# Two up-weight loads moved to GpSimd's queue, and the 384-column output store to ScalarE's

## Chip, core and metric

One Trainium2 chip, one core of it. The metric is the device time of one execution in microseconds (us). In the text, PE is TensorE, ACT is ScalarE, DVE is VectorE, POOL is GpSimd and SP is SyncE; "SPq" in a row of the profile is SP's queue, where it issues a transfer.

## What is computed

A parallel block: a layer norm of `x` (2048 rows of 512), then the sum of `x`, a diagonal state-space layer A and a gated feed-forward layer B. All inputs are bf16, accumulation is in f32.

```python
def reference(A_x, ..., B_w_gate, B_w_up, B_w_down):
    x = A_x
    xn = _layernorm(x, axis=-1)
    ...
    # A: Bu = xn @ B_bar.T ; h_t = Lam_bar * h_(t-1) + Bu_t over 2048 steps ; y = 2 Re(h @ C.T) + xn * Dskip
    # B: (gelu(xn @ w_gate) * (xn @ w_up)) @ w_down, with 512 -> 1376 -> 512
    return x + A(xn) + B(xn)
```

## The kernel before

**Tiling.** The 2048 rows are four blocks `b` of 512, each of four tiles `j` of 128 rows. The feed-forward width of 1376 is eleven tiles of 128 (the last has 96), the model width of 512 is four steps `k` of 128. Per block the kernel forms the normalised transposed rows `XNT`, gate and up products with gelu (`GU`, L842), the state inputs (`BU`, L748), the scan on DVE (`CHAIN`), and the down product together with the states' output product (`DN`, L883).

**Order of the work.** The program records every operation with an assumed duration and the buffers it reads and writes. A planner (`Sched`) then places operations: PE and SP keep the order in which they were recorded, DVE, ACT and POOL are ordered by a simulation of the assumed durations and by explicit `order_behind` links. `emit` writes each engine's list out with semaphore waits; each transfer has a semaphore of its own.

**The first block is special.** It does not wait for transposed normalised rows. Tile by tile, DVE subtracts the mean (`cent`, L960: 128 columns, then 384; for tiles 2 and 3 `sub`, L949), PE transposes the centred tile (`cent_T`, L683), ACT copies it out of PSUM (L688), and PE multiplies it, one `k` step at a time, with the first 512 columns of the gate and up weights (`GT_k`, L700). So the first 512 columns come in eight loads of 128 KB, one for gate and one for up per step `k` (`ld_wk`, L485 to L488, issued in the loop at L500 to L504): here they are called G0, U0, G1, U1, G2, U2, G3, U3, after the step counted from 0. The "steps 2 and 3" of the change's name are U1 and U2 in this count. PE's order at the start is written out by hand (L966 to L1012): transposes of tile 0, transposes of tile 1, tile 0 with G0, with U0, tile 1 with G0, with U0, tile 0 with G1, tile 0 with U1, transposes of tile 2, and so on.

**Queues at the start.** SP issues, one behind the other: `x` tile 0, G0, U0, G1, U1, G2, U2, `x` tile 3, G3, U3, then four larger loads with the other columns of the gate and up weights (L505, L506, L529, L530), a small transpose of the parameters (L514) and the transposes of the normalised rows (L735). ACT issues `x` tiles 1 and 2 and three parameter rows. POOL issues no transfer; it fills constants: an index matrix for the identity (L474), a zero row block (L476), and in the order of the plan a 4-column constant (L541), the index row `IOTJ` of 512 int32 (L477, read by DVE's tables much later), and more constants (L543, L544, L542). DVE makes the identity (`IDN`, L475).

**The end.** The last tile of 128 rows is made in two parts of 384 and 128 columns (`DN(3, tail=384)`, L911 to L920). For each part DVE adds the skip term on the way out of PSUM (`evO`, L901), and SP issues the store (L903). Before the 384-column store SP waits for the landing of all but the last four stores (L336 to L338), and behind the last store for those four (L342, L343).

Of the kernel before, what the change touches and what calls it, by code (L numbers as in the profile page):

```python
# [77 lines left out]
class Sched:  # L78
# [212 lines left out]
    def emit(self):  # L291
        nc, es = self.nc, self.es
        order = self.order
        esem = {}
        for e in ENGINES:
            if any(op.kind == "eng" for op in order[e]):
                esem[e] = es.enter_context(nc.semaphore("q_" + e))
        cnt = {e: 0 for e in ENGINES}
        nd = 0
        for e in ENGINES:  # L300
            for op in order[e]:
                if op.kind == "eng":
                    cnt[e] += 1
                    op.sem, op.val = esem[e], cnt[e]
                else:
                    op.sem, op.val = es.enter_context(nc.semaphore("d%d" % nd)), 16
                    nd += 1
        self.n_sems = len(esem) + nd
        plan = {}
        nwait = 0  # L310
        for e in ENGINES:
            seen = {}
            prog = []
            for op in order[e]:
                need = {}
                for d in op.deps:
                    if d.eng == e and (d is op.behind or d.kind == "eng" and e == "tensor"):
                        continue
                    key = ("e", d.eng) if d.kind == "eng" else ("d", d.id)
                    if seen.get(key, 0) >= d.val:  # L320
                        continue
                    if key not in need or need[key].val < d.val:
                        need[key] = d
                for key, d in need.items():
                    seen[key] = d.val
                waits = [(d.sem, d.val) for d in need.values()]
                nwait += len(waits)
                prog.append((waits, op))
            plan[e] = prog
        self.n_waits = nwait  # L330
        final_waits = [(op.sem, 16) for op in sorted(self.out_ops, key=lambda o: o.finish)]

        for e in ENGINES:
            h = getattr(nc, e)
            for n, (waits, op) in enumerate(plan[e]):
                if e == "sync" and n == len(plan[e]) - 2:  # L336
                    for (s, v) in final_waits[:-4]:
                        h.wait_ge(s, v)  # L338
                for (s, v) in waits:
                    h.wait_ge(s, v)  # L340
                op.fn(h).then_inc(op.sem, 1 if op.kind == "eng" else 16)
        for (s, v) in final_waits[-4:]:  # L342
            nc.sync.wait_ge(s, v)  # L343


# [13 lines left out]
def d_dve_ts4x(n): return 220.0 + 0.26 * n  # L359
D_TINY = 160.0  # L360
def d_act(n, ptr=0): return 190.0 + 0.833 * n + 90.0 * ptr
# [3 lines left out]
def build(nc, ins, out):  # L365
    with ExitStack() as es:
        E = es.enter_context
        S = Sched(nc, es)
# [10 lines left out]
        WU = A.alloc("WU", [KD, F], BF16)  # L379
# [5 lines left out]
        WUc = [Buf("WUc%d" % i, "sbx", 100 + 10 * i, 101 + 10 * i) for i in range(KD + 2)]  # L385
# [34 lines left out]
        PROW = A.alloc("PROW", [128], BF16)  # L420
        PROW16 = Buf("PROW16", "sb", PROW.lo, PROW.hi, PROW.ap[0:16, :])
        PROWq = [Buf("PROW%d" % q, "prow", q, q + 1) for q in range(3)]
# [31 lines left out]
        IOTJ = A.alloc("IOTJ", [512], I32, at=OUTB_all.lo)  # L454
# [11 lines left out]
        POOL = lambda fn, dur, r, w, tag="", after=(): S.op("gpsimd", fn, dur, r, w, tag, after)  # L466
        PE = lambda fn, dur, r, w, tag="": S.op("tensor", fn, dur, r, w, tag)

        GATE = {"before_gelu": [], "nh": 0}
# [3 lines left out]
        GATE["table"] = ACT(lambda e: e.activation(SCR.ap, HALF.ap[:, 0:1], ACTF.Gelu_apprx_tanh), 100, [HALF], [SCR], "gelu0")  # L473
        POOL(lambda e: e.iota(IOT.ap, [[1, 128]], base=0, channel_multiplier=-1), 300, [], [IOT], "iota")  # L474
        GATE["ident"] = V(lambda e: e.tensor_scalar(IDN.ap, IOT.ap, 0.0, None, ALU.is_equal), d_dve_ts4x(128), [IOT], [IDN], "ident")  # L475
        POOL(lambda e: e.memset(PROW16.ap, 0.0), 100, [], [PROW, *PROWq], "prow0")  # L476
        GATE["iotj"] = POOL(lambda e: e.iota(IOTJ.ap, [[1, 512]], base=0, channel_multiplier=0), 600, [], [IOTJ], "iotj")  # L477
        NM0, NM1 = (A.alloc(n, [1], F32) for n in ("NM0", "NM1"))

        def ld_x(b):  # L480
# [1 line left out]
                X_all.ap[:, 4 * b:4 * b + 4, :], x2[512 * b:512 * (b + 1), :].rearrange("(j p) d -> p j d", p=128)),  # L482
                512 * 1024, writes=X[4 * b:4 * b + 4], tag="ld_x%d" % b)

        def ld_wk(W, Wc, src, k):  # L485
            f0, f1 = FC[0]
            return S.dma(lambda e: e.dma_start(W.ap[:, k, f0:f1], src[128 * k:128 * (k + 1), f0:f1]),  # L487
                         256 * (f1 - f0), writes=[Wc[k]], tag="ld_w")  # L488

        def ld_w(W, Wc, src, n):  # L490
            f0, f1 = FC[n]
            return S.dma(lambda e: e.dma_start(W.ap[:, :, f0:f1], src[:, f0:f1].rearrange("(k p) f -> p k f", p=128)),
                         1024 * (f1 - f0), writes=[Wc[KD + n - 1]], tag="ld_w")

        def ld_x0(j, queue="sync", after=()):
            return S.dma(lambda e, j=j: e.dma_start(X[j].ap, x2[128 * j:128 * (j + 1), :]), 128 * 1024, writes=[X[j]], tag="ld_x0", queue=queue, after=after)  # L496
# [3 lines left out]
        for k in range(KD):  # L500
            if k == 3:
                ld_x0(k)
            ld_wk(WG, WGc, ins["B_w_gate"], k)
            ld_wk(WU, WUc, ins["B_w_up"], k)  # L504
        ld_w(WG, WGc, ins["B_w_gate"], 1)  # L505
        ld_w(WU, WUc, ins["B_w_up"], 1)  # L506

# [39 lines left out]
        def next_bank():  # L547
            b_ = rstate["n"] % 8
            rstate["n"] += 1
            return b_  # L550
# [316 lines left out]
        def DN(b, split=False, tail=None):  # L867
            k2, k3 = b % 2, b % 3
            banks = [next_bank() for _ in range(4)]
            xbank = next_bank() if tail else None  # L870

            def seed(j, c0=0, c1=D):
                tt, bank = 4 * b + j, banks[j]
                bank = banks[j] if c0 == 0 else xbank
                ACT(lambda e: e.activation(PS[bank][:, c0:c1], X[tt].ap[:, c0:c1], ACTF.Copy), d_act(c1 - c0), [X[tt]], [BANK[bank]], "seed")  # L875

            def mms(j, ops, last, rds, c0, c1):
                bank = banks[j] if c0 == 0 else xbank

                def f(e):  # L880
                    ins_ = None
                    for n, (l_, r_) in enumerate(ops):
                        ins_ = e.matmul(PS[bank][:, c0:c1], l_[:, 128 * j:128 * (j + 1)], r_[:, c0:c1], start=False,  # L883
                                        stop=last and n == len(ops) - 1, skip_group_check=True)
                    return ins_
                PE(f, d_pe([c1 - c0] * len(ops)), rds + [BANK[bank]], [BANK[bank]], "DN%d" % b)

            def hidden(j, c0=0, c1=D):
                ops = [(HTt[k2][ft].ap[0:FROWS[ft], :], WD.ap[0:FROWS[ft], ft, :]) for ft in range(KF)]
                mms(j, ops, False, [HTt[k2][ft] for ft in range(KF)] + WDc, c0, c1)  # L890

            def states(j, c0=0, c1=D):
                ops = [(SSc[k3][s][c].ap, CT[c][s].ap) for s in range(KP) for c in range(2)]
                mms(j, ops, True, [SSs[k3][s] for s in range(KP)] + [CT[c][s] for c in range(2) for s in range(KP)], c0, c1)

            def store(j, c0=0, c1=D):
                tt = 4 * b + j
                bank = banks[j] if c0 == 0 else xbank
                ko = tt % 4
                ob = OUTB[ko] if c1 - c0 == D else Buf("OUTBp%d" % c0, "sb", OUTB[ko].lo + 2 * c0, OUTB[ko].lo + 2 * c1)  # L900
                V(lambda e: e.tensor_tensor(OUTB[ko].ap[:, c0:c1], PS[bank][:, c0:c1], XD[tt].ap[:, c0:c1], ALU.add),  # L901
                  d_dve_1x(c1 - c0), [BANK[bank], XD[tt]], [ob], "evO")
                S.dma(lambda e: e.dma_start(out[0, 128 * tt:128 * (tt + 1), c0:c1], OUTB[ko].ap[:, c0:c1]),  # L903
                      256 * (c1 - c0), reads=[ob], is_output=True, tag="st_out")

            if split:
                for j in range(4):
                    seed(j); hidden(j)
                for j in range(4):
                    states(j); store(j)  # L910
            elif tail:  # L911
                for j in range(3):
                    seed(j); hidden(j)
                for j in range(3):
                    states(j); store(j)
                parts = ((0, tail), (tail, D))
                for c in parts:
                    seed(3, *c)
                for c in parts:
                    hidden(3, *c); states(3, *c); store(3, *c)  # L920
            else:
                for j in range(4):
                    seed(j); hidden(j); states(j); store(j)
# [183 lines left out]
```

## Time and profile before

| what | us |
|---|---|
| median of 3 runs (lowest, highest) | 177.25 (176.7, 177.45) |
| the profiled execution | 177.24 |
| its span, first to last instruction | 175.9 |
| outside the span (177.24 - 175.9) | 1.3 |
| PE busy | 171.8 (98%) |
| DVE busy | 159.6 (91%) |
| ACT busy | 95.7 (54%) |
| POOL busy | 10.7 (6%) |

The profile is one execution on the chip. Its page gives busy times per engine, the span cut in 40 slices, the queues of the transfers, and the chain of work that ended last, which is followed back from the last instruction to whatever released each step. The trace behind the page answers narrower questions: the instructions of one stretch of time, who waited for whom, and the transfers that were issued in a stretch with the time to their landing. PE is busy for 98% of the span, so time can only be gained where PE stands idle (before its first real matmul and in short gaps), behind its last matmul, or by giving it less work.

### The profile page before, as it was taken

Reading aid. Unit: us, or ns where it says so; the run is one execution under the profiler, and the core shown is the slowest. Engines: PE = TensorE matmul, PEld = TensorE weight load, DVE = VectorE, ACT = ScalarE, POOL = GpSimd, SP = SyncE. Lnnn points to the kernel's source line nnn. Section 1 sums busy time; section 2 is a strip of 40 time slices with the busy share of each in tenths; the row PEclk is TensorE's granted clock in tenths of the full one; section 3 lists DMA queues with packets and bytes.
Section 4 is the critical chain, followed back from the end, with each engine's and each line's share of the span. In section 5 each row is a group of like instructions: output and inputs, shape, how many; then the busy total and the mean of one; then the engine's idle time right before and its main releaser. Section 6 shows DMA issues by size and latency. Waiting matters only on the chain.

```text
span 175.9 us, 2506 instructions
## 1 busy us (share of the span) xinstructions
PE 171.8 (98%) x874; PEld 84.5 (48%) x889; DVE 159.6 (91%) x279; ACT 95.7 (54%) x187; POOL 10.7 (6%) x24
## 2 busy tenths in 40 slices
PE   8899999999999999999999999999999999999995
PEld 2545464844544444444644444444464444444453
DVE  5977999997989989889899999989999899999931
ACT  5376677999766898383576792000667960000000
POOL 3212120210000000002100000000000000000000
DMA  5999999695999000002025000002001000000221
GB/s 174 259 314 186 248 212 121 120 133 108 182 287 232 10 0 2 0 30 88 5 42 109 0 0 0 4 0 89 30 0 30 4 0 0 0 0 0 95 95 56
DMA packets 32421, 14.37 MB, mean 82 GB/s; under 512 B 23736, under 2 KB 32408, under 8 KB 32408
## 3 DMA queue, kind: packets, MB, share of 16 engines
q1 hardware_dynamic: 32096, 13.94, 35.6%
q10 hardware_dynamic: 312, 0.27, 0.5%
q8 instruction: 7, 0.11, 0.3%
q14 instruction: 6, 0.05, 0.1%
HBM read 6.46 MB, written 2.10 MB: 49 GB/s over the span
## 4 chain that ended last, share of the span: by engine, by line
PE 95%; DMA 2%; SPq 1%; issue 1%; DVE 0%
PE PS L883 37%; PE PS L842 32%; PE PS L748 16%; PE PS L711 4%; PE PS L816 3%; PE PS L700 2%; DMA arena<-in_B_w_up_dram 2%; SPq L487 1%; PE PS L683 0%; SPq L496 0%; DVE arena L901 0%
## 5 line engine op out<-in xcount | busy, mean ns | idle before, releaser
L883 PE MATMUL PS<-arena 128*128 128x512 bf16 (+3 forms) x317 | 65.9, 366 | 0.3
L842 PE MATMUL PS<-arena 128*128 128x512 bf16 x257 | 57.1, 379 | 0.4
L883 PEld LDWEIGHTS PS<-arena 128*128 128x128 bf16 (+1 forms) x323 | 30.9, 98 | 35.2
L842 PEld LDWEIGHTS PS<-arena 128*128 128x128 bf16 x264 | 25.7, 98 | 30.3
L786 DVE TENSOR_TENSOR_SCAN arena<-arena 128x512 bf16<-128x512 f32 x32 | 38.9, 1254 | 0.0
L857 ACT ACTIVATE arena<-PS 128x512 bf16<-128x512 f32 x33 | 19.8, 599 | 26.2 <-DVE arena L901 16.7
L748 PE MATMUL PS<-arena 128*128 128x512 bf16 (+1 forms) x142 | 28.1, 355 | 0.1
L861 ACT ACTIVATE arena<-PS 128x512 bf16<-128x512 f32 x33 | 19.8, 599 | 5.4 <-PE PS L842 5.4
L748 PEld LDWEIGHTS PS<-arena 128*128 128x128 bf16 x144 | 14.1, 98 | 13.3
L875 ACT ACTIVATE PS<-arena 128x512 f32<-128x512 bf16 (+2 forms) x17 | 9.6, 581 | 19.7 <-DVE arena L901 19.0
L757 ACT ACTIVATE arena<-PS 128x512 bf16<-128x512 f32 x32 | 17.5, 596 | 1.8 <-PE PS L748 1.8
L901 DVE TENSOR_TENSOR arena<-PS,arena 128x512 bf16<-128x512 f32 (+2 forms) x17 | 10.9, 652 | 6.4 <-PE PS L883 6.3
L863 DVE TENSOR_TENSOR arena<-arena 128x512 bf16<-128x512 bf16 x33 | 13.2, 416 | 2.2 <-ACT arena L861 2.0
L775 DVE TENSOR_TENSOR arena<-arena 128x4096 bf16<-128x4096 bf16 (+1 forms) x5 | 9.2, 1859 | 0.4 <-ACT arena L610 0.4
L798 DVE TENSOR_TENSOR arena<-arena 128x4096 bf16<-128x4096 bf16 x4 | 9.2, 2288 | 0.1
L773 DVE TENSOR_TENSOR arena<-arena 128x4096 bf16<-128x4096 bf16 (+1 forms) x5 | 9.2, 1857 | 0.0
L799 DVE TENSOR_TENSOR arena<-arena 128x4096 bf16<-128x4096 bf16 x4 | 9.1, 2284 | 0.0
L720 ACT ACTIVATE arena<-PS,arena 128x256 bf16<-128x256 f32 (+1 forms) x16 | 6.5, 450 | 4.1 <-PE PS L700 2.4
L614 DVE BATCH_NORM_STATS2 arena<-arena 128x6 f32<-128x512 bf16 x12 | 7.8, 680 | 0.0
L711 PE MATMUL PS<-arena 128*128 128x512 bf16 (+1 forms) x40 | 7.1, 336 | 0.0
L723 DVE SCALAR_TENSOR_TENSOR arena<-PS,arena 128x256 bf16<-128x256 f32 (+1 forms) x16 | 6.3, 443 | 0.8 <-PE PS L700 0.8
L700 PE MATMUL PS<-arena 128*128 128x512 bf16 (+1 forms) x30 | 6.1, 337 | 0.5 <-DMA arena<-in_B_w_up_dram 0.5
(95 smaller groups left out, 123.6 us busy)
## 6 DMA issues: line engine op xcount, KB each, us to landing
out_dram<-arena SPq DMA_DIRECT2D x15, 128.0 KB, 1.7
arena<-in_A_x_dram SPq DMA_DIRECT2D x3, 512.0 KB, 5.5
arena<-in_B_w_down_dram SPq DMA_DIRECT2D x1, 1280.0 KB, 8.8
arena<-in_B_w_gate_dram SPq DMA_DIRECT2D x4, 128.0 KB, 3.3
arena<-in_B_w_up_dram SPq DMA_DIRECT2D x4, 128.0 KB, 3.6
arena<-in_B_w_gate_dram SPq DMA_DIRECT2D x1, 480.0 KB, 6.8
arena<-in_B_w_up_dram SPq DMA_DIRECT2D x1, 480.0 KB, 7.7
arena<-arena SPq DMA_TRANSPOSE x25, 2.9
```

Source lines behind the costliest of these rows:

```text
L700: PE(lambda e: e.matmul(dst, XCd(j, k), WGU[:, ws[0]:ws[-1] + 1, k, f0:f1], start=first, stop=k == KD - 1, skip_group_check=True), d_pe([w ...
L711: ins_ = e.matmul(dst, XCd(j, k), WGU[:, :, k, f0:f1], start=(k == 0), stop=(k == KD - 1))
L748: ins_ = e.matmul(PS[bank][:, 128 * j0:128 * j1], BBT[c][dk].ap[:, 128 * s:128 * (s + 1)], XNT[b].ap[:, dk, 128 * j0:128 * j1], start=(dk ...
L757: GATE["evBu"] = ACT(lambda e, bank=bank, k3=k3, s=s, c=c: e.activation(SSc[k3][s][c].ap, PS[bank][:, :], ACTF.Copy), d_act(512), [BANK[ba ...
L786: V(lambda e, g=g, rb=rb, init=init: e.tensor_tensor_scan(g.ap, rb, g.ap, init, ALU.mult, ALU.add), d_dve_scan(512), [g, PA[RRr]] + ([CARc ...
L842: ins_ = e.matmul(PS[bank][0:m, c0:c1], W.ap[:, dk, 128 * ft:128 * ft + m], XNT[b].ap[:, dk, c0:c1], start=(dk == 0), stop=(dk == KD - 1))
L857: GATE["last_gelu"] = ACT(lambda e, bg=bg, kk=kk, m=m: e.activation(GG[kk].ap[0:m, :], PS[bg][0:m, :], ACTF.Gelu_apprx_tanh), d_act(512), ...
L861: ACT(lambda e, bu=bu, kk=kk, m=m: e.activation(UPB[kk].ap[0:m, :], PS[bu][0:m, :], ACTF.Copy), d_act(512), [BANK[bu]], [UPB[kk]], "evU")
L863: V(lambda e, kk=kk, m=m, ft=ft, k2=k2: e.tensor_tensor(HTt[k2][ft].ap[0:m, :], GG[kk].ap[0:m, :], UPB[kk].ap[0:m, :], ALU.mult), d_dve_tt ...
L875: ACT(lambda e: e.activation(PS[bank][:, c0:c1], X[tt].ap[:, c0:c1], ACTF.Copy), d_act(c1 - c0), [X[tt]], [BANK[bank]], "seed")
L883: ins_ = e.matmul(PS[bank][:, c0:c1], l_[:, 128 * j:128 * (j + 1)], r_[:, c0:c1], start=False, stop=last and n == len(ops) - 1, skip_group ...
L901: V(lambda e: e.tensor_tensor(OUTB[ko].ap[:, c0:c1], PS[bank][:, c0:c1], XD[tt].ap[:, c0:c1], ALU.add), d_dve_1x(c1 - c0), [BANK[bank], XD ...
```

## The change

Three things are edited. No instruction of PE or DVE is added, removed or reordered.

1. U1 and U2 are issued from POOL's queue, behind the zero row block (L476) and in this order, instead of from SP's. In the changed program POOL's list is: index matrix, zero row block, load U1, load U2, the 4-column constant, the index row `IOTJ`, and the other constants. SP's list loses two entries near its front: `x` tile 0, G0, U0, G1, G2, `x` tile 3, G3, U3, and so on.
2. The store of the 384-column part is issued from ACT's queue, where it is the last instruction. The 128-column store stays on SP.
3. SP's waits for landed stores are split anew: before its last store but one (a full tile of the last block) it waits for the first 12 of the 17 stores, before its last store (128 columns) for the next three, each set closed by a no-op, and behind the last store there is one instruction that waits for both parts of the last tile.

```diff
@@ emit
-                if e == "sync" and n == len(plan[e]) - 2:
-                    for (s, v) in final_waits[:-4]:
+                if e == "sync" and n >= len(plan[e]) - 2:
+                    for (s, v) in (final_waits[:-5] if n < len(plan[e]) - 1 else final_waits[-5:-2]):
                         h.wait_ge(s, v)
+                    h.nop(nofuse=True)
                 for (s, v) in waits:
                     h.wait_ge(s, v)
                 op.fn(h).then_inc(op.sem, 1 if op.kind == "eng" else 16)
-        for (s, v) in final_waits[-4:]:
+        for (s, v) in final_waits[-2:]:
             nc.sync.wait_ge(s, v)
@@ build
-        POOL(lambda e: e.memset(PROW16.ap, 0.0), 100, [], [PROW, *PROWq], "prow0")
-        GATE["iotj"] = POOL(lambda e: e.iota(IOTJ.ap, [[1, 512]], base=0, channel_multiplier=0), 600, [], [IOTJ], "iotj")
+        GATE["swdge"] = POOL(lambda e: e.memset(PROW16.ap, 0.0), 100, [], [PROW, *PROWq], "prow0")
...
-        def ld_wk(W, Wc, src, k):
+        def ld_wk(W, Wc, src, k, queue="sync"):
             f0, f1 = FC[0]
             return S.dma(lambda e: e.dma_start(W.ap[:, k, f0:f1], src[128 * k:128 * (k + 1), f0:f1]),
-                         256 * (f1 - f0), writes=[Wc[k]], tag="ld_w")
+                         256 * (f1 - f0), writes=[Wc[k]], tag="ld_w", queue=queue)
...
             ld_wk(WG, WGc, ins["B_w_gate"], k)
-            ld_wk(WU, WUc, ins["B_w_up"], k)
+            if k == 0:
+                ld_wk(WU, WUc, ins["B_w_up"], k)
+            else:
+                op_ = ld_wk(WU, WUc, ins["B_w_up"], k, "gpsimd" if k < 3 else "sync")
+                if k < 3:
+                    GATE["swdge"] = S.order_behind(op_, GATE["swdge"])
+        S.order_behind(POOL(lambda e: e.iota(IOTJ.ap, [[1, 512]], base=0, channel_multiplier=0), 600, [], [IOTJ], "iotj"), GATE["swdge"])
...
                 S.dma(lambda e: e.dma_start(out[0, 128 * tt:128 * (tt + 1), c0:c1], OUTB[ko].ap[:, c0:c1]),
-                      256 * (c1 - c0), reads=[ob], is_output=True, tag="st_out")
+                      256 * (c1 - c0), reads=[ob], is_output=True, tag="st_out", queue="scalar" if c1 - c0 == tail else "sync")
```

## The prediction

> **What bounds the kernel now.** I read the chain that ended last first, because PE is busy for 98% of the span and only what stands outside PE's work can be saved. These are the two ends of that chain; the columns are start, duration and what ran.
>
> ```profile
> 1.66 0.42 SPq L487
> 2.08 0.04 issue
> 2.12 0.43 SPq L487
> 2.56 0.04 issue
> 2.60 3.94 DMA arena<-in_B_w_up_dram
> 6.54 0.05 issue
> 6.58 0.39 PE PS L700 x2
> ...
> 173.91 0.02 issue
> 173.93 0.29 DVE arena L901
> ```
>
> Until 6.58 the end of the kernel hangs on U1, issued at 2.60 and landed at 6.54; after it the chain is PE without a break to 173.91, then the last `evO` and its store. PE's timeline shows how much there is at the front: eight matmuls from 5.00 (four steps of two), then a stop.
>
> ```profile
> 5.00 1.10 PE L700 MATMUL PS<-arena 128*128 128x256 bf16 x8
> 6.58 0.39 PE L700 MATMUL PS<-arena 128*128 128x256 bf16 x2 [0.48 <-DMA arena<-in_B_w_up_dram]
> ```
>
> The eight end at 6.10, the last of them lasts 0.27 and so starts at 5.83. Two neighbours stand 0.12 apart (6.58 to 6.97, the second also 0.27 long), so the U1 step could have begun at 5.95. **At most 6.58 - 5.95 = 0.63 us is to be had there.** Next the tail, SP's queue beside DVE's last two additions (mean ns behind the bar):
>
> ```profile
> 173.97 0.33 SPq L903 DMA_DIRECT2D out_dram<-arena  x1
> ```
> ```profile
> 174.35 0.42 SPq L903 DMA_DIRECT2D out_dram<-arena  x1
> ```
> ```profile
> L901 DVE TENSOR_TENSOR arena<-PS,arena 128x384 bf16<-128x384 f32 x1 | 0.6, 558 | 2.8 <-PE PS L883 2.8
> L901 DVE TENSOR_TENSOR arena<-PS,arena 128x128 bf16<-128x128 f32 x1 | 0.3, 293 | 0.1
> ```
>
> The 128-column sum is ready at 173.93 + 0.29 = 174.22, but SP is issuing the 384-column store until 174.30 and starts the last one at 174.35.
>
> **The tail, worked out.** An unhindered store follows its addition closely: the store at 170.59 follows an addition that ran from 169.87 for 0.69, so 0.03 behind. The last store could start at 174.22 + 0.03 = 174.25 instead of 174.35: **0.10 us earlier**, and the end of the span, its landing 1.5 later, with it. ACT's new last instruction has nothing behind it, and ACT's row before ends at 162.72 + 0.28 = 163.00, so nothing is delayed. That store leaves at 173.87 + 0.03 = 173.90 and lands 1.6 later (the 96 KB row), 175.5, ahead of the last at 174.25 + 1.5 = 175.75; ACT's loads at the start took 2.3 where SP's took 2.2, which does not close the 0.25. The waits cost nothing on either side: before the last store they ask for three stores of which the latest left at 170.59 and lands 1.7 later, at 172.3, 1.9 us before it matters. The closing wait that goes lay in the 1.5 us of landing. Bounds: 0 to 0.10; I take 0.10, since the row at 170.59 is the same kind of store on the same queue.
>
> **The front, worked out.** SP's issues stand 0.47 apart (2.12, 2.60, 3.08). So G1 keeps 2.12, G2 moves from 3.08 to 2.60, `x` tile 3 from 4.03 to 3.08, G3 and U3 and the larger loads forward by two issues, 0.95. None of these was awaited: U2 landed at 3.55 + 3.7 = 7.25 for a step that PE starts about 8.3, U3 at 4.98 + 3.5 = 8.5 for one at 9.6 (the 7th and the 13th of the matmuls that stand 0.22 apart from 7.04). The transposes behind them gain little, since L735 waits for DVE's normalised rows (9.11 + 0.41 = 9.52, now issued at 9.74).
>
> U1 itself leaves POOL behind the zero block (1.01 + 0.20 = 1.21), not at 2.60. That is not 1.39 us of gain, because the transfers were not waiting for issue. Here are the busy tenths of the DMA engines in 0.2 us slices from 0 to 8:
>
> ```profile
> DMA  0000000005699999999998999986788999997699
> ```
>
> From 2.2 us on they are full. Landings follow one another at the pace of the transfers: U0 at 1.66 + 3.3 = 4.96, G1 at 2.12 + 3.2 = 5.3, G2 at 3.08 + 3.8 = 6.9, U2 at 7.25, so about 0.37 per 128 KB. U1 alone is out of step, 1.2 behind G1, of which 0.83 is excess. Without it U1 would have landed at 6.54 - 0.83 = 5.71. In the changed kernel U2 is in flight early too and takes its 0.37 before the four loads U0, G1, U1, U2 are through, so the last of what PE needs, now probably G1 on SP's queue, lands at 5.71 + 0.37 = 6.08. PE then does G1's two matmuls (0.22) and, 0.04 behind the landing as before, reaches U1's step at 6.08 + 0.04 + 0.22 = 6.34: **0.24 earlier**. From 6.58 on PE's own work follows without gaps, and things that PE does not feed have more room than that: `sub` of tile 3 ends at 8.56 + 0.35 = 8.91 for a transpose at 9.84, the fourth transpose of L735 lands about 13.8 + 2.9 = 16.7 for products at 18.29.
>
> The price of a POOL issue is not in this trace. Below, ACT's shortest issue is 0.27 and SP's 0.43; above, the longest issue at the start is SP's transpose with 2.03. I take 0.87, POOL's own costliest instruction (L621), because it is POOL that has to do the work: U1 is issued by 2.08, U2 by 2.95, and the constants that took POOL from 1.21 to 2.36 now run from 2.95 to 4.11. POOL's next need is at 7.58, after 5.2 us of idle time, and the index row's reader starts at 17.3, so lateness on POOL itself is free up to 4 us. If an issue were as cheap as SP's, constants end at 3.2; at 2.03, at 6.4.
>
> What may not be free is DVE. While POOL filled its constants before, this stood on DVE, against 254 ns for the 128-column form of L960:
>
> ```profile
> 1.10 1.23 DVE L475 TENSOR_SCALAR arena<-arena 128x128 bf16<-128x128 int32 x1
> ```
>
> It ended with POOL's run (2.33 against 2.36). Later, L949 took its usual 0.35 at 8.56 beside two POOL instructions of one or three columns. So wide POOL fills may hold such an operation up, small ones did not. In the changed kernel the fills meet the `cent` operations (3.48 to 3.96, 4.17 to 4.65), which feed PE: a hold until 4.11 puts them and all of PE's start 0.63 late, and U1's step to 5.95 + 0.63 = 6.58, no gain at all. I take no hold for the forecast, as the type of L475 differs from that of `cent`.
>
> The Trainium skill speaks against this change in two places. "SBUF — State Buffer", Who interferes with whom, says that a DVE operation in a two-port mode (`tensor_scalar` can be one) and a POOL operation exclude each other, and that a transfer issued from GpSimd waits for its descriptors meanwhile; L475 agrees with it and L949 at 8.56 does not show it. By that rule the hold above would be the forecast, 177.14. "DMA: Bandwidth & Descriptors", Issuing engines are not separate DMA queues, says that another issuer saves issue time alone; by that rule only the order at the engines counts, and the front gives 0 to 0.24.
>
> **Sum.** 177.24 (profiled, 175.9 of span and 1.3 around it; the median is 177.25) - 0.24 - 0.10 = **176.90**.
>
> **Rivals.**
> - *The wait moves to another load, or the hold eats the gain.* U1 and U2 get ahead, G1 or U0 is late; or the fills hold `cent` for 0.63. The excess of 0.83 can strike G1 as well as U1. For it: full DMA engines, a fixed number of bytes. Time: 177.24 - 0.10 = 177.1, within 0.2.
> - *POOL holds DVE for longer (the other side).* Its place is the first `cent` at 3.48, and it decides from a hold of 0.63 on. A whole constant run of 1.16 in front of it gives 5.95 + 1.16 = 7.11 for U1's step: 177.24 + 0.53 - 0.10 = 177.7. With issues of 2.03 that keep DVE out until 1.21 + 4.06 = 5.27, the hold is 1.79 and the time 177.24 + 1.16 - 0.10 = 178.3. For it: L475. Against it: 5.27 needs both the dearest issue and a hold by work that no row shows.
> - *The whole stop goes.* U1 early, G1 by 5.6: 0.63 + 0.10, 176.5. Against it: G1 would have to land as before although two more loads compete.
> - *The change does nothing at the front* because POOL's transfers start late: with 2.03 for each issue U1 leaves POOL at 3.24 and lands, with the 3.5 us that such loads took at the start, at 6.7: 177.24 + 0.2 - 0.10 = 177.3.
>
> **Chances.** Forecast (176.7 to 177.05) 0.40; the stop gone 0.15; no net gain at the front (177.05 to 177.4, with POOL's late start) 0.25; POOL in DVE's way, up to 178.1, 0.10, and beyond 0.10. A measurement of this kernel can tell about 0.5%, 0.9 us, from no change (its three runs differ by 0.75). Even the whole 0.73 stays inside that; with scatter, 0.04 for faster by over 0.5%. Slower by over 0.5% is the last case, 0.10; within 0.5% 0.86. The range runs from 176.4, the whole gain and a little scatter, to 177.9, which leaves out the worst of POOL's case.
>
> **What would show it.** Right: PE's first L700 step on U1 begins between 6.0 and 6.5 with the remaining stop put down to a gate load, and SP's last store starts 0.03 behind `evO`. Wrong: a stop before the first L683, or L960 rows well over 254 and 314 ns (hold); POOL's issue rows over 2 us; the last landing that of ACT's store; or a stop that now comes later, at the transposes of tile 3.

## The result, and the profile after

| | before | changed |
|---|---|---|
| median of 22 runs (lowest, highest) | 177.27 (176.7, 179.28) | 178.47 (177.66, 187.0) |
| ratio, 95% interval | | 1.006 (1.004 to 1.0081) |
| median span / median time outside the span (before: over the 34 runs beside the repeat below) | 175.95 / 1.31 | 176.75 / 1.74 |

The median rose by 1.2 us, where 0.34 less was predicted. Four of the changed kernel's runs were slow ones with TensorE's clock below full; the ratio leaves them out, and without them its median is 178.28, 1.0 above before. The first profiled execution of the changed kernel (180.36 us) had TensorE at half speed for a stretch and is far off its median, so most lines below come from another execution of the same code, 178.53 us with a span of 176.8, which lies close to the median. Line numbers have moved by up to six: L700, L711, L901 and L960 of before are L706, L717, L907 and L966 (the experiments' kernels have their own shifts). Its chain of work that ended last, the front of it (start, duration, what ran):

```profile
1.66 5.01 DMA arena<-in_B_w_up_dram
6.66 0.05 issue
6.71 1.26 PE PS L706 x10
7.97 0.22 PE PS L689 x4
8.20 2.81 PE PS L706 x13
```

The load at the head was issued at 1.66: that is **U0**, which stayed on SP's queue, not U1. It takes 5.01 to its landing, against 3.3 before. From there on PE runs without a break to the end, as before from 6.58. PE's timeline says the same:

```profile
4.64 0.38 PE L706 MATMUL PS<-arena 128*128 128x256 bf16 x2
4.85 0.33 PE L689 MATMUL PS<-arena 128*128 128x128 bf16 x3
6.71 1.26 PE L706 MATMUL PS<-arena 128*128 128x256 bf16 x10 [1.53 <-DMA arena<-in_B_w_up_dram]
...
12.14 1.03 PE L717 MATMUL PS<-arena 128*128 128x512 bf16 x4
```

Before, eight matmuls ran from 5.00 and the stop of 0.48 came behind them, at U1. Now PE stops for 1.53 ahead of U0, and the ten matmuls that follow find all they need, U1 among it. The two loads on POOL's queue, and POOL's timeline (the work on POOL went as foreseen):

```profile
1.39 1.27 POOL L487 DMA_DIRECT2D arena<-in_B_w_up_dram  x2 [0.18 <-issue]
2.65 0.12 POOL L547 MEMSET arena<- 128x4 f32 x1
2.70 0.58 POOL L510 IOTA arena<- 128x512 int32 x1
3.20 0.13 POOL L549 MEMSET arena<- 128x1 f32 x1
3.23 0.55 POOL L550 MEMSET arena<- 128x512 bf16 x1
```

The transfers of the first 8 us in the same execution, in 0.2 us slices, and the three queues that moved them (q1 is SP's, q10 ACT's, q0 POOL's):

```profile
DMA  0000000019789999886998897995999989999989
...
q1 hardware_dynamic: 1409, 1.25, 54.8%
q10 hardware_dynamic: 312, 0.27, 10.7%
q0 software_dynamic: 96, 0.26, 10.5%
```

The engines are as full as before. What changed is whose bytes they carry. The trace's packet records give GB/s per queue (a packet counts where it starts):

```
                     3.5-4.0  4.0-4.5  4.5-5.0  5.0-5.5 us
before   q1 (SP)       217      285      262      221
changed  q1 (SP)        94       96      115      137
changed  q0 (POOL)      90      123      156      123
```

In these 2 us SP's queue moves 221 KB instead of 492 KB (the sum of a row times 0.5), and POOL's takes 246 KB, nearly all of its two loads. Of U0's sixteen parts the first lands at 4.11 (4.04 before), but the ninth at 5.04 and the last at 6.67 (4.40 and 4.96 before).

The tail, SP's and ACT's queue, and the end of the chain:

```profile
174.90 0.38 ACTq L909 DMA_DIRECT2D out_dram<-arena  x1
```
```profile
175.25 0.33 SPq L909 DMA_DIRECT2D out_dram<-arena  x1
```
```profile
174.91 0.02 issue
174.93 0.29 DVE arena L907
```

The last addition ends at 175.22 and the last store starts at 175.25, 0.03 behind it, as foreseen.

**The difference, added up** (this execution against the profiled one before): the last addition ends at 175.22 instead of 174.22, **+1.00**; from there to the end of the span it is 1.58 instead of 1.72, **-0.14**; outside the span 178.53 - 176.8 = 1.73 instead of 1.3, **+0.43**. The sum is +1.29, and 178.53 - 177.24 = 1.29.

### The profile page after: what moved, and what is told of

It is laid out like the page before. It is cut to its first block, busy times and chain, and to the rows that moved or that the text cites. A ratio compares the mean times of both kernels' runs of the same rounds, so it can differ in the third digit from the quotient of the medians.

```text
span 178.6 us, 2506 instructions
## 1 busy us (share of the span) xinstructions
PE 173.2 (97%) x874; PEld 85.4 (48%) x889; DVE 158.8 (89%) x279; ACT 95.9 (54%) x187; POOL 12.2 (7%) x26
## 4 chain that ended last, share of the span: by engine, by line
PE 95%; DMA 3%; issue 1%; SPq 0%; DVE 0%
PE PS L889 37%; PE PS L848 32%; PE PS L754 15%; PE PS L717 4%; PE PS L706 4%; PE PS L822 3%; DMA arena<-in_B_w_up_dram 3%; PE PS L689 0%; SPq L487 0%; SPq L496 0%; DVE arena L907 0%
## 5 line engine op out<-in xcount | busy, mean ns | idle before, releaser
L754 PE MATMUL PS<-arena 128*128 128x512 bf16 (+1 forms) x142 | 28.1, 355 | 0.1
L907 DVE TENSOR_TENSOR arena<-PS,arena 128x512 bf16<-128x512 f32 (+2 forms) x17 | 10.9, 651 | 6.4 <-PE PS L889 6.3
L706 PE MATMUL PS<-arena 128*128 128x512 bf16 (+1 forms) x30 | 7.4, 403 | 1.7 <-DMA arena<-in_B_w_up_dram 1.7
L717 PE MATMUL PS<-arena 128*128 128x512 bf16 (+1 forms) x40 | 7.1, 336 | 0.0
```

The costliest lines, as they stand in the source:

```text
L706: PE(lambda e: e.matmul(dst, XCd(j, k), WGU[:, ws[0]:ws[-1] + 1, k, f0:f1], start=first, stop=k == KD - 1, skip_group_check=True), d_pe([w ...
L717: ins_ = e.matmul(dst, XCd(j, k), WGU[:, :, k, f0:f1], start=(k == 0), stop=(k == KD - 1))
L754: ins_ = e.matmul(PS[bank][:, 128 * j0:128 * j1], BBT[c][dk].ap[:, 128 * s:128 * (s + 1)], XNT[b].ap[:, dk, 128 * j0:128 * j1], start=(dk ...
```

## The experiments

The theory (A): POOL's two transfers take part of the engines ahead of U0 and G1, which PE needs first; PE starts late by that much, and some 0.45 us outside the span comes with POOL's queue. Its rivals: any second issuer does it; the new tail costs it; the charge outside belongs to something else; a fall of PE's clock, or a stretch later than the front, holds the rest.

Each was compared with the kernel before on the same chip; "outside" is time less span, a median over the runs. Where no interval is given, it was one execution.

**The changed kernel again**, without an edit.

> The changed kernel once more. Theory A (POOL's transfers hold up U0, the second up load on SP's queue, and the stop that follows sometimes makes the clock drop): U0 lands 1 us or more behind its 4.96 of before, PE stops about 1 to 1.8 us at U0's step; time 177.7 to 178.7 without a half-clock stretch in the trace, near 180 with one (the profiled execution had 0.5 from 6.94 to 10.36). Rival B (a chance of that one profiled execution, the loss sits elsewhere): U0 lands near 5.0 in this trace and the time is lost at another place.

Measured: 178.55, ratio 1.0072 (1.0047 to 1.0096), span 176.8, outside 1.75. The loss stands. Its profiled execution was one of the quicker (177.86): U0 landed at 5.57, less late than theory A's 1 us, with its step at 5.62, then came a second stop at G1 (6.67):

```profile
5.62 0.83 PE L706 MATMUL PS<-arena 128*128 128x256 bf16 x6 [0.44 <-DMA arena<-in_B_w_up_dram]
6.67 0.61 PE L706 MATMUL PS<-arena 128*128 128x256 bf16 x4 [0.23 <-DMA arena<-in_B_w_gate_dram]
```

**The tail alone.** U1, U2 and the index row as before; the store on ACT and the new waits kept.

```diff
-            if k == 0:
...
-                op_ = ld_wk(WU, WUc, ins["B_w_up"], k, "gpsimd" if k < 3 else "sync")
...
+            ld_wk(WU, WUc, ins["B_w_up"], k)
```

> Only the tail of the change: the 384-column store on ACT and the split waits; all eight weight loads on SP and POOL as before. Theory A: all of the loss is at the front, so the time is 0.0 to 0.10 us under before (177.15 to 177.25), with the last store issued 0.03 behind its addition. Rival C (the tail loses too, by ACT's store landing late or by SP's waits): 177.4 or more, with the last landing that of ACT's store.

Measured: 177.30, ratio 0.9993 (0.9973 to 1.0013), outside 1.34. The tail costs nothing; all of the loss belongs to the loads on POOL. Its profiled execution has 1.60 from the last addition to the end of the span, against 1.72 before, so 0.12 is saved there; the timing can't resolve that. In this execution (176.45, span 175.1) PE had no stop at the front at all, although the loads stood in the order of before: U0 landed at 4.72 and U1 at 5.71.

```profile
4.86 1.32 PE L701 MATMUL PS<-arena 128*128 128x256 bf16 x10
```

**U1 and U2 from ACT instead.** The tail's edit, the two loads on ACT's queue, the parameter rows moved from ACT to SP.

```diff
+            if k in (1, 2):
+                GATE["par"] = S.order_behind(ld_wk(WU, WUc, ins["B_w_up"], k, "scalar"), GATE["par"])
...
```

> U1 and U2 on ACT's queue behind x tiles 1 and 2 instead of on POOL's; the three parameter rows go to SP behind U3 so that ACT's first activation is not pushed back; the tail as changed. Theory A (it is POOL's queue, with its packets of 4096 bytes against 1024 and a slow start, that holds U0 up): U0 lands by 5.4, PE's stop at U0 is under 0.45 us, time 176.9 to 177.3. Rival D (any second queue that carries two loads past U0 costs the same): U0 lands at 5.7 or later, time 177.7 to 178.4.

Measured: 177.14, ratio 0.9994 (0.9977 to 1.0012), outside 1.31. A second issuer as such doesn't cost what POOL cost. Nor does it gain: U1's step no longer waits, but the ten matmuls in a row begin only at 5.53, since U0 landed at 5.49 (4.96 in the profile before; theory A had said by 5.4):

```profile
5.01 0.53 PE L684 MATMUL PS<-arena 128*128 128x128 bf16 x3
5.53 1.33 PE L701 MATMUL PS<-arena 128*128 128x256 bf16 x10
```

**The parameter rows alone on SP**, with the tail's edit.

```diff
...
-                      1024, writes=[PROWq[q]], tag="ld_" + nm, queue="scalar", after=[half]), GATE["par"])
...
+                      1024, writes=[PROWq[q]], tag="ld_" + nm, after=[half])
```

> The control for the run with U1 and U2 on ACT: the three parameter rows on SP behind U3 and the changed tail, all weight loads on SP in the old order, no POOL transfer. Theory A: as with the tail alone, 177.1 to 177.3, so that what the ACT version gains or loses is due to U1 and U2. Rival H (the tiny rows on ACT's queue were what made single engines late for U1): U1 lands by 5.9 and the time is 176.5 to 176.9.

Measured: 177.24, ratio 0.9994 (0.9979 to 1.0009), outside 1.28. The move that the ACT version needed does nothing to the median by itself. In the profiled execution U1 landed at 6.29, so rival H falls, and U0 landed at 5.70; PE stopped there and not at U1:

```profile
5.74 1.27 PE L698 MATMUL PS<-arena 128*128 128x256 bf16 x10 [0.66 <-DMA arena<-in_B_w_up_dram]
```

So with U1 and U2 left on SP, U0's landing scatters from one execution to the next: 4.72, 4.96 (before), 5.44 (the run with a late POOL load below) and 5.70, and the load that PE waits for changes with it. The stop of 0.48 at U1, on which the prediction was built, is that of one execution. U0's 5.49 in the ACT version and 5.57 in the 177.86 execution lie within this scatter, the 5.95 to 6.78 of the changed kernel's other executions beyond it; what shows the loss is the median of the span, 176.75 and 176.8 for the changed kernel against 175.7 to 176.0 for every kernel with U0 in its old place and no POOL load at the front.

**Only U2 on POOL.**

```diff
-                op_ = ld_wk(WU, WUc, ins["B_w_up"], k, "gpsimd" if k < 3 else "sync")
+                op_ = ld_wk(WU, WUc, ins["B_w_up"], k, "gpsimd" if k == 2 else "sync")
```

> Half the dose: U1 back on SP, only U2 from POOL; the rest as changed. Theory A with the slow start of POOL's transfers as the main part: U0 still lands 0.8 us or more late, time 177.6 to 178.3. Theory A with the bytes of the larger packets as the main part: U0 about half as late as in the changed kernel, 0.6 to 0.9, time 177.3 to 177.7. Rival D (bytes alone, 0.37 a load): U0 at most 0.4 late, time 177.1 to 177.3.

Measured: 177.95, ratio 1.0044 (1.0018 to 1.007), span 176.1, outside 1.82. With half the early POOL traffic the span grows by 0.15 rather than 0.8, but the time outside it grows by the full 0.5. In the profiled execution U0 landed at 6.03, and the stop still falls ahead of it, though U2 is needed two steps later:

```profile
6.07 1.27 PE L706 MATMUL PS<-arena 128*128 128x256 bf16 x10 [0.49 <-DMA arena<-in_B_w_up_dram]
```

**One POOL transfer far from the front.** The tail's edit; an `x` load of the last block, needed much later, goes to POOL, all weights to SP.

```diff
+        ld_x(3, "gpsimd", [GATE["evBu"]])
```

> All weight loads on SP as before, the tail as changed, and one transfer that nobody awaits (the last 512 KB of x, read at about 80 us) from POOL's queue behind the block-1 work, at 40 us or later. In the runs so far the kernels with a POOL transfer stand 1.74 to 1.82 us outside the span, those without 1.31. Theory F (any POOL transfer at all costs that 0.45, wherever it stands): 1.75 outside the span, span as with the tail alone (175.8 to 176.0), time 177.6 to 177.8. Rival G (the 0.45 belongs to POOL transfers at the start): 1.31 outside the span, time 177.15 to 177.3.

Measured: 177.57, ratio 1.0016 (0.9999 to 1.0033), span 175.7, outside 1.84. The load was issued at 40.7 and nobody waited for it:

```profile
L482 POOL DMA_DIRECT2D arena<-in_A_x_dram x1: 917/917/917, 40.7 to 40.7; - x1
```

Yet the time outside the span is 0.5 up. **This charge comes with the use of POOL's queue, not with place, count or size:** one load of 512 KB at 40.7, one of 128 KB at the front or two of them all give 1.7 to 1.85, and every kernel without such a load 1.28 to 1.35 (medians; single runs lie at 1.67 to 1.90 and at 1.25 to 1.37). What happens in it was not seen.

**G3 and U3 on POOL**, behind its fills; U1 and U2 back on SP.

```diff
+        fl = S.order_behind(ld_wk(WG, WGc, ins["B_w_gate"], 3, "gpsimd"), fl)
+        fl = S.order_behind(ld_wk(WU, WUc, ins["B_w_up"], 3, "gpsimd"), fl)
```

> POOL carries two loads as in the changed kernel, but the two that are needed last (G3 and U3, at 9.4 us), issued behind its index row and its widest constant, at about 2.3 us; U1 and U2 are back on SP. Theory A (the loss in the span comes from U0 and G1 sharing the engines with POOL's packets): POOL's packets begin at 4.5 or later, U0 lands by 5.1, the span's median is 175.7 to 176.1, and with 0.45 outside it the time is 177.4 to 177.8. Rival E (POOL's queue slows the first block wherever its loads stand): the span's median is 176.5 or more, time 178.2 or more.

Measured: 177.88, ratio 1.0034 (1.0015 to 1.0054), span 176.15, outside 1.72. Two loads on POOL that start later cost 0.15 of span instead of 0.8, and the same 0.4 outside. That is just above theory A's ranges and below rival E's. The one profiled execution took 179.68, far above the median, so where the 0.15 falls can't be read from it. In it POOL's packets ran from 4.19 on, U0 landed at 6.08 where A had said by 5.1, and TensorE ran at half speed: two matmuls took 0.62 and the ten 2.31, against 0.38 and 1.26 in the 178.53 execution.

```profile
4.74 0.62 PE L704 MATMUL PS<-arena 128*128 128x256 bf16 x2
6.13 2.31 PE L704 MATMUL PS<-arena 128*128 128x256 bf16 x10 [0.46 <-DMA arena<-in_B_w_up_dram]
```

**U0 issued behind U2.** The tail's edit, all loads on SP.

```diff
+            if k > 0:
                 ld_wk(WU, WUc, ins["B_w_up"], k)
...
+            if k == 2:
+                ld_wk(WU, WUc, ins["B_w_up"], 0)
```

> No POOL transfer, the tail as changed, and U0 put behind U2 on SP's queue, so that PE stops for about 2.3 us at U0's step (U0 issued at 3.55, landing near 7.2). Theory I (a stop of well over a microsecond makes the clock drop for one stretch of 3.4 us, as in the profiled execution of the changed kernel): a granted clock of 0.5 for 3.41 us behind the stop, and the time 177.2 + 1.7 to 2.3 for the stop + 1.7 for the clock, 179.5 to 181. Rival J (the drop in that execution was chance): the clock stays at 1.0 and the time is 178 to 179.

Measured: 178.63, span 177.3, outside 1.33. A late U0 alone, with no POOL transfer, reproduces a loss of this size in the span:

```profile
4.56 0.61 PE L704 MATMUL PS<-arena 128*128 128x256 bf16 x2
7.04 1.27 PE L704 MATMUL PS<-arena 128*128 128x256 bf16 x10 [1.54 <-DMA arena<-in_B_w_up_dram]
```

PE's stop in front of U0 is 1.54 by the timeline (the 2.1 of a later expectation runs from 4.97, the start of the three matmuls ahead). The two matmuls before the stop ran at half speed (0.61), the ten behind it at full (1.27). The speed did not fall behind the stop of 1.53 in the 178.53 execution either; it did behind one of 1.68 in the first profiled one, and in the execution with G3 and U3 on POOL it was low both before and behind a stop of 0.46. So the length of the stop alone does not tell whether a half-speed stretch comes.

**Three more executions of the changed kernel**, to see whether the rest of the loss also stands at the front.

> The changed kernel, a further single execution with its trace. The regular trace of it has a span of 176.1, while the median span of its 33 runs is 176.8. Theory A (the loss inside the span is PE's late start alone, because U0 and G1 land late beside GpSimd's transfers): the span stands at 176.1 - 11.43 = 164.67, plus or minus 0.2, behind the start of the first transpose of tile 3 of the first block (L711), whatever the span of this execution is; a span of 176.8 has L711 at 12.1, with U0 landing at 5.9 or later, or G1 later than 6.9. Rival K (a later stretch is longer too, as GpSimd's constants or its two transfers move something else): a span of 176.8 has L711 at 11.4 to 11.6, and the rest is found behind 11.5.

> The changed kernel, another single execution. As for the look before: theory A has the span 164.67 plus or minus 0.2 behind the start of L711; rival K has a span that grows while L711 stays at 11.4 to 11.6.

> The changed kernel, another single execution. As for the look before: theory A has the span 164.67 plus or minus 0.2 behind the start of L711; rival K has a span that grows while L711 stays at 11.4 to 11.6.

Measured, with the two executions that came before:

| execution, us | span | U0 landed | PE's U0 step | L717 (L711 before) | span less that |
|---|---|---|---|---|---|
| before, 177.24 | 175.9 | 4.96 | 5.00 | 11.12 | 164.78 |
| 177.86 | 176.1 | 5.57 | 5.62 | 11.43 | 164.67 |
| 178.22 | 176.5 | 6.29 | 6.33 | 11.80 | 164.70 |
| 178.53 | 176.8 | 6.67 | 6.71 | 12.12 | 164.68 |
| 179.84 | 178.1 | 5.95 | 6.03 | 13.37 | 164.73 |
| 180.36 | 178.6 | 6.78 | 6.82 | 13.90 | 164.70 |

In the five executions of the changed kernel the last column is the same to 0.06, whatever the span. Everything that differs between them inside the span has happened before the transposes of tile 3, and rival K falls. In the first three it is U0's landing, with some at G1. In the last two a second thing comes on top. In the execution of 179.84 G0 was late too, and the matmuls ran at half speed before the stop as well as behind it: two took 0.61 (0.38 in the 178.53 execution), the ten 2.34 (1.26). Its page lists a full clock, but its trace holds no record of the clock, so the durations decide:

```profile
5.41 0.61 PE L706 MATMUL PS<-arena 128*128 128x256 bf16 x2 [0.69 <-DMA arena<-in_B_w_gate_dram]
5.81 0.52 PE L689 MATMUL PS<-arena 128*128 128x128 bf16 x3
6.13 2.34 PE L706 MATMUL PS<-arena 128*128 128x256 bf16 x10
```

In every trace here PE begins at this speed: the first 512-column matmuls, on constant data, start 0.43 us apart, later ones 0.22. The change came by 7.04 us at the latest in the other traces, but at about 9.6 in this one and in that of G3 and U3 on POOL. In the execution of 180.36 PE had been at full speed already (two matmuls in 0.38 at 4.60) and fell back; the same ten took 2.24, and there the granted clock shows it. The columns are the stretch, then busy times, PE's clock, the share of the transfer engines and GB/s:

```profile
3.50:7.00 3.50, 1.56 (x14) 0.90 (x14) 2.54 (x8) 1.97 (x6) 0.46 (x2) 0.99 0.95 267
7.00:10.40 3.40, 3.40 (x17) 2.18 (x16) 3.16 (x12) 0.77 (x2) 1.90 (x4) 0.51 1.07 364
```

**U0 late, and PE kept busy.** As above with U0 behind U2, and 44 matmuls on constant data ahead of PE's U0 step.

```diff
+        fill(44)
         ks(0, 0, [1])
```

> The kernel with U0 recorded behind U2, and 44 more matmuls on constant data ahead of PE's first step on U0, which leave nothing out and change no result. Without them PE stood idle for 2.1 us, the clock was granted in full, L711 started at 12.45 and the last addition ended at 175.55. Theory L (an idle PE costs more than its stop, as a later stretch is slower behind it): with PE busy the last addition comes closer to L711, 163.4 to 163.7 behind it instead of 163.1 is the same, below 163.0 is a gain; the time is 178.2 or less. Rival M (only the stop counts): L711 at 12.4 to 12.9 and the time 178.5 to 179.0.

Measured: 179.45, span 178.1, outside 1.35. Theory L gets no support from this one execution: L715 starts at 12.86, and the last addition ends at 176.61, 163.75 behind it rather than below 163.0. M's starting time holds, its total (178.5 to 179.0) does not, because a wait comes that neither theory had:

```profile
PE PS L715 <- DVE arena L727: 0.5, 1, 0.5
```

The chain leads from it to the parameter transpose on SP's queue, which took 6.90 from 8.02 on. The clock question stays open: both executions with U0 behind U2 ran at full speed from U0's step on, so they have no stretch for the filling to remove.

## Why the prediction was wrong, by its steps

- **The tail was right.** 0.10 by the rows, 0.14 and 0.12 in two traces; the last store follows its addition by 0.03. (From the last addition to the end of the span, twelve of the thirteen traces with the new tail have 1.51 to 1.63 against 1.72; that of U0 behind U2 has 1.71.)
- **POOL's issue and the fills were right in kind.** 0.63 each on the mean (542 and 722 ns) where 0.87 was taken, and the fills ran from 2.65, not 2.95. (SP's shortest issue at the start was 0.40, not the 0.43 given; nothing hangs on it.)
- **The hold on DVE came, and cost nothing.** The prediction took no hold, because `cent`'s type differs from L475's. In the five traces of the changed kernel the first `cent` operation took 327 to 512 ns instead of 254, the longer the earlier it began (3.33 to 3.51), and ended at 3.83 to 3.84 in each, just behind POOL's 512-column fill (3.23 + 0.55 = 3.78). With only U2 on POOL that fill ended at 3.22, and `cent` took 254 again. In the execution of 179.84:

```profile
3.33 0.51 DVE L966 TENSOR_SCALAR arena<-arena 128x128 bf16<-128x128 bf16 x1
3.23 0.55 POOL L550 MEMSET arena<- 128x512 bf16 x1
```

That is the sign of a hold that the prediction named (rows well over 254 ns). The term of zero was right by luck: the fill ended at 3.78 and not at 4.11, and PE had U0 to wait for anyway. The identity shows the same hold from the other side: with the index row moved behind the loads, L476 took 0.23 where L475 took 1.23 before, and 1.23 again in the run with the tail alone, where the index row stood as before. The section of "SBUF — State Buffer" that the prediction weighed (Who interferes with whom), by which these two engines exclude each other in two-port modes, agrees with both rows; in which mode the operations ran, no row tells.

- **The front failed**, at the step "the last of what PE needs, now probably G1 on SP's queue, lands at 5.71 + 0.37 = 6.08". Its bytes were counted rightly: the engines were full, and a load costs about 0.37. But it summed four loads to one last landing and supposed that those ahead in time stay ahead. U0, first in need, was left where it had been (4.96). The runs show it at 5.57 to 6.78, against 4.72 to 5.70 in four executions with U1 and U2 on SP: POOL's queue got some half of the bandwidth from 3.5 to 5.5 for data that PE needs later. U1 came early (5.85 in the 178.53 execution) and was worth nothing. Instead of -0.24 the front gave +1.00 in the execution close to the median. The base was weak too: the stop at U1 and its excess of 0.83 were read from one execution, and others with the same order of loads had no stop, or one at U0.
- **The rival "the wait moves to another load" had the mechanism** and U0's name, but not the size: it let the excess of 0.83 strike another load, so that the gain was merely eaten, 177.1. It did not ask what it costs that the load that is hit is needed a microsecond sooner (5.00) than the one that is relieved (5.95).
- **The other side had the wrong place.** It was sought in DVE, where a row (L475) had caught the eye, and not in the transfers, although the prediction's own row had shown that the engines were full.
- **The time around the span was carried over unchanged** (1.3), the second term at fault: 1.74. No row of the trace before could show it, since it had no POOL transfer; an unknown of that kind belonged in the range, on the upper side.

Added up from the prediction's terms: -0.10 became -0.14, -0.24 became +1.00, and 0 became +0.43.

The rule that the prediction cited from "DMA: Bandwidth & Descriptors", Issuing engines are not separate DMA queues, was the nearer guide, as far as it goes: another issuer added no bandwidth. Its bound for the front, 0 to 0.24 of gain, was drawn from it too kindly. The same page's section SWDGE vs HWDGE vs iDMA says that each transfer engine has internal queues which GpSimd's and the other issuers' work feed separately, and that it takes them in turn; the nearly equal shares of q0 and q1 above fit that. That turns taken in packets of 4 KB against 1 KB favour POOL is a guess, which no run here isolates.

What is shown and what is not: that the front's loss is U0's and G1's lateness, by the table of executions and by `u0_late`; that it comes with POOL's early transfers and not with another issuer or with the tail, by the medians of the runs with each alone. Two 128 KB loads in front of U0 and G1 would explain 2 x 0.37 = 0.74 of lateness at most; U0 was late by up to 1.8, and why single parts of it land so much later than the others, and why U0 scatters by 1.0 even with the loads in the old order, stays open. So does what the 0.45 outside the span is, and when the half-speed stretch comes.

No version beat the kernel before by more than the measurement can tell: the best three stand at 0.9993 and 0.9994, with 1 inside their intervals.

## What to carry to other kernels

When transfer engines are full, moving a load to another queue can move bandwidth, not only issue time (here two loads on POOL's queue cost 0.8 us of span, the same two on ACT's nothing): write down the order in which the loads are needed, and ask of every load ahead of the moved one what happens if its bytes now share with it. A wait that goes at the fourth load can come back larger at the second. Before building on a stop of half a microsecond, look whether a second execution has it in the same place. And a queue that a kernel hasn't used before can have a price that no row shows; measure it by one idle transfer on that queue before the design depends on it.

## What the runs showed of the hardware beyond that

- A kernel with any transfer from POOL's queue took 1.72 to 1.84 outside its span in the median, the others 1.28 to 1.35.
- POOL's queue moved its loads in packets of 4096 bytes (159 ns in the median), SP's and ACT's 128 KB loads in packets of 1024 (46 ns): 26 and 22 bytes per ns, so the packet itself is not slower. POOL's first data packet started 2.0 to 2.4 us behind the start of its issue in the changed kernel (3.39 to 3.76 for one at 1.39), 1.8 for the load at 40.7 (42.52).
- TensorE ran at half clock for one stretch of 3.41 us (6.94 to 10.36) in the execution of 180.36, behind 3.5 us in which PE had been busy for 1.56. "TensorE: Matmul & The Clock Gate", Part 1, gives a free-running window of 3413 ns: the length agrees, though PE was not idle for the whole of it.
- A 128-column `cent` operation of DVE beside a 512-column fill of POOL ended only behind the fill, 0.07 to 0.26 us longer than its usual 0.25.
